# First two quads of a fused attention and MoE kernel as eight plain block products in two halves of tokens

## The chip, the cores and the metric

The kernel runs on one core of a Trainium2 chip. The metric is device time in microseconds (us), the median of three runs. The engines are named as in the profile: PE (TensorE, matrix products) with PEld (its weight loads), DVE (VectorE), ACT (ScalarE), POOL (GpSimd) and SP (SyncE, which here issues nearly all transfers).

## The reference

Three stages follow each other: attention with pooled keys and values, a dense mixture of four experts, and a gated layer with a norm. The inputs q, k, v have the shape (4, 8, 576, 64); there are 2304 tokens of width 512.

```python
def _attn_ref(q, k, v):
    k_p = k.reshape(B, H, Sp, pool, D).mean(axis=3)      # pool = 8, Sp = 72
    v_p = v.reshape(B, H, Sp, pool, D).mean(axis=3)
    scores = scale * np.matmul(q, k_p.transpose(0, 1, 3, 2))
    attn = softmax(scores)          # written out in the reference
    return np.matmul(attn, v_p)

def _moe_ref(x, domain_probs, w1, w2):   # E, F = 4, 1024
    p = domain_probs / (domain_probs.sum(-1, keepdims=True) + 1e-09)
    for e in range(E):
        h = np.maximum(x @ w1[e], 0.0)
        out += p[:, e:e + 1] * (h @ w2[e])

def _moe2_ref(x, w_gate, w_val, w_out, rms_g):   # d_ff = 1536
    xn = x / rms * rms_g
    g = xn @ w_gate
    return (g * sigmoid(g) * (xn @ w_val)) @ w_out
```

(The softmax and the sigmoid are shortened here.)

## The kernel before

**Tokens.** The 2304 tokens are 18 tiles of 128, worked on in three passes of six tiles. Each pass has two halves of N = 384 tokens, A and B.

**Products.** Every float32 operand is split into a high part (rounded by ScalarE to the format fp32r) and a low part (the rest, by VectorE), and a product is three matmuls: high by high, high by low, low by high (L462 to L464).

**Quads.** A quad is one block of 256 inner columns of an expert's first layer: 16 a pass. The 512 x 256 weights and the 768 tokens of a pass are each cut into 2 x 2 blocks (weights B11, B12, B21, B22; tokens a11 and a12 are the two halves of the width for token half A, a21 and a22 for B). `quad` (L441) makes the quad with seven block products instead of eight, by the table `STEPS`: sums of operands (s1 to s4 of tokens, T1, T2, N3, N4 of weights) go in, and sums of products come out. A product is six matmuls 128x384, so a quad is 42. The sums of tokens are made by `x_ops` once a pass, those of weights by `prep_w` (L253) once a quad, on GpSimd. After the products `relu_after` writes the hidden layer h of either half, high and low again.

**Second layer.** `second` (L777) takes a pair of quads and makes, for each of the six token tiles, 12 matmuls 128x512 with the pair's two rows of w2 (`prep_w2`, L308). These 72 are taken in pieces of three as a side queue between the products of the next quads.

**Hooks.** After each of a quad's seven products a hook runs: it takes the next piece of the side queue, the next step of the weight preparation, a tick that lets due stores go, and `att_step`, which runs the attention work written for this step. `when(i)` gives the step at which tile i of passes 1 and 2 begins; a tile's scores with exponentials (`att_a`), normalisation (`att_b`), transposes (`att_c`) and value products (`att_d`) follow at 0, 4, 8 and 13 steps from there. In that phase they all use one PSUM buffer of two banks (tag "at").

**First pass.** The attention of pass 0's six tiles runs before any quad, in the order 0, 3, 1, 4, 2, 5, with dummy products (`heat`) on TensorE. Its PSUM pool (two score buffers, three transpose banks, one dummy bank) is released before the quads' pool is opened. The token operands are made in thirds of columns, a third when both tiles of it (one of each half) are there.

The order of the instructions on each engine is the order of the program text; there is no scheduler.

Of the kernel before, what the change touches and what calls it, by code (L numbers as in the profile page):

```python
# [54 lines left out]
def tile_kernel(ctx: ExitStack, tc, qp, kp, vp, dp, w1r, w2r, w64, rg, out):  # L55
# [61 lines left out]
    def x_ops(c0=0, c1=N, new=True):  # L117

        a11, a12, a21, a22 = (xr[o, d][:, :, c0:c1] for o in (0, N) for d in range(2))

        if new:
            for _, _, _, name in STEPS:
                new_xo(name)

        def high(name, src):
            nc.scalar.activation(xo[0][name][:, 0, :, c0:c1], src, AF.Copy)

        def low(name, src):
            t = xo[0][name]
            nc.vector.tensor_tensor(t[:, 1, :, c0:c1], src, f32(t[:, 0, :, c0:c1]), op=ALU.subtract)  # L130
# [3 lines left out]

        add(a21, a11, ALU.subtract)
        high("a11", a11)
        yield
        low("a11", a11)
# [4 lines left out]
        high("a22", a22)  # L143
        yield
        add(a11, a21, ALU.add)
        high("s2", a21)
        high("a12", a12)
        yield
        low("s2", a21)
        low("a22", a22)  # L150
        high("s1", a11)
        yield
        low("a12", a12)
        low("s1", a11)
        add(a12, a21, ALU.subtract)
# [4 lines left out]
        yield  # L160
# [135 lines left out]


# [143 lines left out]
    def quad(i, after):  # L441
# [8 lines left out]
        seeded = i > 0  # L450
# [29 lines left out]
    def new_h(half, key):  # L480
        t = late["sb"].tile([P, 2, 2, N], F32R, name="h" + half, tag="h" + half, bufs=4 if half == "A" else 3)
        h_t[half, key] = t
        return t

# [292 lines left out]
    def second(keys, first, last):  # L777

        k, p, e, _ = keys[0]
        for t in (3, 4, 5, 0, 1, 2):  # L780
# [103 lines left out]
    def load_q(i):  # L884
# [8 lines left out]
        nc.sync.dma_start(t, qp[i].rearrange("p (j s) -> p j s", j=NPAIR))  # L893
# [9 lines left out]
    def pool_k(b, j, stage=None, eng=None):  # L903
# [41 lines left out]
    def heat(k):  # L945

        if "heat" not in at:
            at["heat"] = at["ps"].tile([P, 512], F32, name="heat")
        for _ in range(k):
            nc.tensor.matmul(at["heat"][:, :P], ident, ident, start=True, stop=True)  # L950
# [41 lines left out]
    def att_c(i):  # L992
# [6 lines left out]
        both = at["ps"].tile([P, 2, 512], F32, name="tr", tag="at") if at["few"] else None  # L999
        tr = [both[:, a] if at["few"] else at["ps"].tile([P, 512], F32, name="tr", tag="tr", bufs=3) for a in range(2)]  # L1000
        for h in range(H):
            nc.tensor.transpose(tr[h // 4][:SP, h % 4 * P:(h % 4 + 1) * P], es[:, h, :], ident)
        for a in range(2):
            src = tr[a][:SP, :].rearrange("p (h s) -> p h s", h=4)
            if a and not at["few"]:
# [5 lines left out]
    def att_d(i):  # L1011
        aT = aT_t.pop(i)
        if at["few"]:
# [12 lines left out]
        if p == 0:  # L1026
            for d in range(2):
# [312 lines left out]
```

## Time and profile before

| what | us |
|---|---|
| median of three runs | 1278.65 (1277.1 to 1281.29) |
| profiled execution | 1276.43 |
| its span | 1274.1 |
| TensorE busy | 1247.5 (98%) |
| VectorE busy | 828.2 (65%) |
| ScalarE busy | 535.4 (42%) |
| GpSimd busy | 268.7 (21%) |

The busy time of an engine is the union of its instructions. Matmuls are pipelined: the length of one in the trace (0.33 us for 128x384) overlaps the next, and the spacing of starts is what it costs. The span is that of the instructions, and the time of the execution contains a little beside it. PEclk is the clock that TensorE was granted, as a share of 2.4 GHz.

### The profile page before, as it was taken

The page shows a single profiled execution, that of the slowest core. Times are in us where ns is not written, and L with a number is a line of the kernel's source. Part 1 is how long each engine was busy: PE and PEld are TensorE (multiplying, and loading weights), DVE is VectorE, ACT ScalarE, POOL GpSimd, SP SyncE. Part 2 cuts the span into 40 slices and gives each one's busy share as a digit, 9 for nine tenths or more (in the row PEclk, how much of TensorE's full clock was granted, in tenths as well). Part 3 has the DMA queues.
Part 4 walks back from the last instruction along what each step waited for, and adds up shares of the span by engine and source line. Part 5 has one row for each costly group of instructions (what it writes and reads, how often), then busy time and mean ns, then how long its engine had stood idle before and what let it go on. Part 6 is the DMA issues. An engine that isn't in the chain of part 4 may idle for free.

```text
span 1274.1 us, 18396 instructions
## 1 busy us (share of the span) xinstructions
PE 1247.5 (98%) x6872; PEld 1153.5 (91%) x6872; DVE 828.2 (65%) x1340; ACT 535.4 (42%) x1239; POOL 268.7 (21%) x253
## 2 busy tenths in 40 slices
PE   7899999999999999999999999999999999999998
PEld 6788888888988888888889998888999999999998
DVE  5864556557466676645677787475667765786575
ACT  5674444444453333323443333255454433433331
POOL 5335333410031222200242343122220000000000
PEclk8899999999999999999999999999999999999999
DMA  8297777768788786664989998747877776867671
GB/s 248 85 340 278 276 252 248 286 236 313 277 309 281 258 286 255 233 246 168 330 312 332 325 326 314 281 177 274 328 263 277 279 293 254 313 242 295 233 275 50
DMA packets 118937, 339.15 MB, mean 266 GB/s; under 512 B 10304, under 2 KB 48192, under 8 KB 99648
## 3 DMA queue, kind: packets, MB, share of 16 engines
q1 hardware_dynamic: 118512, 336.80, 73.0%
q10 hardware_dynamic: 336, 1.18, 0.3%
q8 instruction: 54, 0.88, 0.3%
q14 instruction: 35, 0.29, 0.1%
HBM read 233.61 MB, written 104.33 MB: 265 GB/s over the span
## 4 chain that ended last, share of the span: by engine, by line
PE 84%; DVE 8%; DMA 4%; ACT 2%; issue 1%; SPq 0%; DVEq 0%; ACTq 0%
PE py L788 9%; PE py L789 9%; PE py L787 9%; PE qX L462 8%; PE qX L464 8%; PE qX L463 8%; PE qY L462 4%; PE qY L463 4%; PE qY L464 4%; PE qZ L462 2%; PE qZ L464 2%; PE qZ L463 2%; DMA wc_d<-cx 2%; PE gy L734 1%; PE gx L667 1%; PE av L1020 1%
## 5 line engine op out<-in xcount | busy, mean ns | idle before, releaser
L799 DVE SCALAR_TENSOR_TENSOR y<-py,dps,y 128x512 f32<-128x512 f32 x126 | 94.4, 749 | 186.4 <-PE py L789 186.3
L377 POOL TENSOR_TENSOR cx<-cx 128x512 f32<-128x512 f32 x36 | 49.8, 1383 | 380.4 <-DVE cx L376 91.2
L462 PE MATMUL qX<-xos,wt 128*128 128x384 f32 x336 | 116.2, 346 | 5.1 <-ACT s L470 3.5
L464 PE MATMUL qX<-xos,wt 128*128 128x384 f32 x336 | 113.6, 338 | 0.0
L789 PE MATMUL py<-w,hB 128*128 128x512 f32 x288 | 113.5, 394 | 0.0
L789 PE MATMUL py<-w,hA 128*128 128x512 f32 x288 | 113.4, 394 | 0.0
L788 PE MATMUL py<-w,hB 128*128 128x512 f32 x288 | 113.3, 393 | 0.0
L788 PE MATMUL py<-w,hA 128*128 128x512 f32 x288 | 113.2, 393 | 0.0
L463 PE MATMUL qX<-xos,wt 128*128 128x384 f32 x336 | 113.1, 337 | 0.0
L787 PE MATMUL py<-w,hB 128*128 128x512 f32 x288 | 112.0, 389 | 0.0
L787 PE MATMUL py<-w,hA 128*128 128x512 f32 x288 | 112.0, 389 | 0.0
L491 ACT ACTIVATE hB<-u 128x768 fp32r<-128x768 f32 x48 | 40.8, 850 | 139.3 <-DVE u L474 139.2
L273 POOL TENSOR_TENSOR tw<-rw 128x512 f32<-128x512 f32 x28 | 41.3, 1474 | 263.0 <-DVE wt L291 192.0
L470 ACT ACTIVATE s<-qX 128x384 f32<-128x384 f32 x85 | 41.6, 490 | 120.3 <-PE qX L464 120.2
L467 ACT ACTIVATE qZ<-qX 128x384 f32<-128x384 f32 x83 | 39.8, 480 | 120.5 <-PE qX L464 82.6
L472 DVE TENSOR_TENSOR u<-qY,s 128x384 f32<-128x384 f32 x84 | 46.5, 553 | 56.5 <-PE qY L464 27.2
L462 PEld LDWEIGHTS qX<-xos,wt 128*128 128x128 f32 x336 | 63.3, 188 | 13.2 <-ACT s L470 5.8
L463 PEld LDWEIGHTS qX<-xos,wt 128*128 128x128 f32 x336 | 63.3, 189 | 2.9
L789 PEld LDWEIGHTS py<-w,hB 128*128 128x128 f32 x288 | 54.0, 188 | 11.5
L789 PEld LDWEIGHTS py<-w,hA 128*128 128x128 f32 x288 | 54.0, 188 | 11.4
L464 PEld LDWEIGHTS qX<-xos,wt 128*128 128x128 f32 x336 | 63.1, 188 | 0.2 <-DVE wt L291 0.2
L788 PEld LDWEIGHTS py<-w,hA 128*128 128x128 f32 x288 | 54.0, 188 | 10.1
(188 smaller groups left out, 3499.4 us busy)
## 6 DMA issues: line engine op xcount, KB each, us to landing
wt<-wt_d SPq DMA_DIRECT2D x56, 1024.0 KB, 7.4
w<-w_d SPq DMA_DIRECT2D x32, 1024.0 KB, 8.6
wt_d<-wt SPq DMA_DIRECT2D x28, 1024.0 KB, 7.3
wr<-wr_d SPq DMA_DIRECT2D x56, 512.0 KB, 8.0
wr_d<-wr SPq DMA_DIRECT2D x28, 768.0 KB, 5.9
cr<-w SPq DMA_DIRECT2D x36, 512.0 KB, 7.1
w<-ws_d SPq DMA_DIRECT2D x18, 1024.0 KB, 5.8
w_d<-w SPq DMA_DIRECT2D x16, 1024.0 KB, 9.0
```

Source lines behind the costliest of these rows:

```text
L273: nc.gpsimd.tensor_tensor(t[:, T1:N3 + 1], r[:, B12:B12 + 1].to_broadcast([P, 2, 256]), r[:, B11:B22 + 1], op=sub)
L377: nc.gpsimd.tensor_tensor(x, x, m.bitcast(F32), op=ALU.mult)
L462: nc.tensor.matmul(bank[b], wh, xh, start=first and k == 0, stop=False, **kw)
L463: nc.tensor.matmul(bank[b], wh, xl, start=False, stop=False, **kw)
L464: nc.tensor.matmul(bank[b], wl, xh, start=False, stop=k == 1, **kw)
L470: nc.scalar.activation(s[n], bank[b], AF.Copy)
L472: nc.vector.tensor_tensor(u[:, 0], bank["Y"], s[2], op=ALU.add)
L491: nc.scalar.activation(h[:, 0], u, AF.Relu)
L787: nc.tensor.matmul(ps, lhs[0], w[:, 0, c], start=j == 0, stop=False)
L788: nc.tensor.matmul(ps, lhs[0], w[:, 1, c], start=False, stop=False)
L789: nc.tensor.matmul(ps, lhs[1], w[:, 0, c], start=False, stop=j == len(units) - 1)
L799: nc.vector.scalar_tensor_tensor(y_t[t], ps, gate, y_t[t], op0=ALU.mult, op1=ALU.add)
```

## The change

Quads 0 and 1 are no longer made by `quad` but by eight plain block products each, four for either half of the tokens, in `by_half(i, h, c)`: quad i, half h, column block c. The plain products need no sums. The tiles of attention come in the order 0 to 5, so that half A is whole after three tiles; `att_d` writes the split operands directly from PSUM. Half A's four products and its second layer (tiles 0, 1, 2 of `second`) are written between the stages of tiles 3 to 5, then come half B's four products, two more tiles of the second layer, and quad 2. The PSUM pool is now opened after the first exponentials of tile 3, and in this stretch transposes and values use the quads' banks qY and qZ ("few" is 2). The token sums are made whole (`x_rest`) and no longer in thirds, the weight sums of quads 0 and 1 in pieces. The small copies of the second batch's pooled keys move from ScalarE to GpSimd. As 14 hooks fewer are left, the pass-1 tiles follow each other after 13 steps instead of 16. The core of the diff:

```diff
+    def by_half(i, h, c):
+        w = wop[i]
+        key = quads[i]
+        o = h_t.get(("AB"[h], key)) if c else new_h("AB"[h], key)
+        ps = late["ps"].tile([P, 512], F32, name="qX", tag="qX", bufs=2)[:, :N]
+        blocks = ((B11, B21), (B12, B22))[c]
+        for j, (name, slot) in enumerate(zip((("a11", "a12"), ("a21", "a22"))[h], blocks)):
+            for k in range(2):
...
+                nc.tensor.matmul(ps, wh, xh, start=j == k == 0, stop=False)
+                nc.tensor.matmul(ps, wh, xl, start=False, stop=False)
+                nc.tensor.matmul(ps, wl, xh, start=False, stop=j == k == 1)
+        def out():
+            nc.scalar.activation(o[:, 0, c], ps, AF.Relu)
+            nc.vector.scalar_tensor_tensor(
+                o[:, 1, c], ps, 0.0, f32(o[:, 0, c]), op0=ALU.max, op1=ALU.subtract
+            )
+        return out
-        seeded = i > 0
+        seeded = i > 2
...
-                    nc.scalar.activation(kpb[b % 2][sl, j + i, hh, :], c[sl], AF.Copy)
+                    if b:
+                        nc.gpsimd.tensor_copy(o, c[sl])
+                    else:
+                        nc.scalar.activation(o, c[sl], AF.Copy)
...
-        if at["few"]:
+        if at["few"] == 2:
+            av = late["ps"].tile([P, 512], F32, name="av", tag="qY")
+        elif at["few"]:
             av = at["ps"].tile([P, 2, 512], F32, name="av", tag="at")[:, 0]
...
+            for d in range(2):
+                nc.scalar.activation(ops[d][:, 0, :, sl], avv[:, 2 * d:2 * d + 2], AF.Copy, scale=1.0 / POOL)
+            for d in range(2):
+                nc.vector.scalar_tensor_tensor(
+                    ops[d][:, 1, :, sl], avv[:, 2 * d:2 * d + 2], 1.0 / POOL, f32(ops[d][:, 0, :, sl]),
+                    op0=ALU.mult, op1=ALU.subtract,
+                )
...
+    by_half(0, 0, 0)()
+    o = by_half(0, 0, 1)
+    att_b(3)
+    att_sc(4)
+    first_high(1)
+    first_low(1)
+    att_c(3)
+    o()
+    gates()
+    att_ex(4)
+    o = by_half(1, 0, 0)
+    att_d(3)
...
+    att_b(4)
+    att_sc(5)
+    o = by_half(1, 0, 1)
...
+    att_ex(5)
+    run(two[:1], 4)
+    load_w2(rows[1])
+    att_d(4)
+    tick()
+    py = second(pair, True, False, range(TT))
+    run(two[1:], 5)
+    att_b(5)
+    for _ in range(4):
+        next(py)
+    att_c(5)
...
-        return (p - 1) * NSTEP + 2 + 16 * t
+        return NSTEP - 12 + 16 * t if p > 1 else 2 + 13 * t
```

The instructions of TensorE where the block products of the first quads begin, in the kernel before: `heat` are dummy products, `tr` the transposes and `av` the value products of the last tiles, `qX` the first product of quad 0.

```order
L950 MATMUL heat<-ident 128x128 x10
L1002 MATMUL tr<-ident,es 72x128 x8
L1020 MATMUL av<-aT,vpb_90 64x128 x8
L1020 MATMUL av<-aT,vpb_93 64x128 x8
L950 MATMUL heat<-ident 128x128 x4
L462 MATMUL qX<-xoa_385,wr 128x384
L463 MATMUL qX<-xoa_385,wr 128x384
```

The same place on TensorE in the changed kernel: the transposes and value products are those of tile 2, the third.

```order
L1076 MATMUL tr<-ident,es 72x128 x8
L1017 MATMUL heat<-ident 128x128 x4
L1096 MATMUL av<-aT,vpb_90 64x128 x8
L1017 MATMUL heat<-ident 128x128 x6
L535 MATMUL qX<-xoa_187,wr 128x384
L536 MATMUL qX<-xoa_187,wr 128x384
```

The first products have moved ahead of the attention of tiles 3 to 5, of which only the scores of tile 3 stand before them.

VectorE in the changed kernel, around the second row of w2: `w_562` and `w_643` are the low parts of the first and second row, `xoa` the low parts of tile 4's operands, L1055 to L1057 tile 5's normalisation, L1080 the copy of its transposes.

```order
L359 TENSOR_TENSOR w_562<-rw_179,w_562 128x512
L1108 SCALAR_TENSOR_TENSOR xoa_194<-av,xoa_194 128x2x128
L1108 SCALAR_TENSOR_TENSOR xoa_190<-av,xoa_190 128x2x128
L359 TENSOR_TENSOR w_643<-rw_616,w_643 128x512 x2
L1055 TENSOR_SCALAR sm<-sm 128x8
L1056 RECIPROCAL sm<-sm 128x8
L1057 TENSOR_TENSOR es<-es,sm 128x576
L1080 COPY aT<-tr 72x512
```

Before, all of the attention of pass 0 stands ahead of the w2 parts on VectorE; now the last tile's normalisation stands behind those of the second row.

TensorE in pass 1 before, where the value products of a tile end: `qX` and `qY` are products of a quad, `py` the second layer.

```order
L1020 MATMUL av<-aT,vpb_93 64x128 x8
L462 MATMUL qX<-xos_387,wt 128x384
L463 MATMUL qX<-xos_387,wt 128x384
L464 MATMUL qX<-xos_387,wt 128x384
L462 MATMUL qX<-xos_387,wt 128x384
L463 MATMUL qX<-xos_387,wt 128x384
```

The same in the changed kernel, at one of five such places: `sc` are the scores of the next tile.

```order
L502 MATMUL qX<-xos_193,wr 128x384
L1096 MATMUL av<-aT,vpb_93 64x128 x8
L1032 MATMUL sc<-kpb_88,q 128x144 x4
L500 MATMUL qX<-xoa_187,wr 128x384
L501 MATMUL qX<-xoa_187,wr 128x384
```

The scores, which stood two products and a piece of the second layer further on, now stand directly behind the value products, both on the buffer "at".

## Rows read from the trace of the kernel before

**Rows 1.** The page: busy time of each engine.
```profile
PE 1247.5 (98%) x6872; PEld 1153.5 (91%) x6872; DVE 828.2 (65%) x1340; ACT 535.4 (42%) x1239; POOL 268.7 (21%) x253
```

**Rows 2.** Windows from 77.76 to 330 us: sum of busy time by engine.
```profile
sum 252.24, PE 252.08 PEld 225.41 DVE 145.29 ACT 118.70 POOL 77.56; mean PE 36.01 PEld 32.20 DVE 20.76 ACT 16.96 POOL 11.08
```

**Rows 3.** TensorE timeline: start, length (us), line, operation; the quads' first matmuls.
```profile
50.64 1.16 PE L950 MATMUL heat<-ident 128*128 128x128 f32 x8
...
54.08 0.69 PE L462 MATMUL qX<-xoa,wr 128*128 128x384 f32 x1 [2.28 <-ACT xoa L126]
...
66.32 0.33 PE L462 MATMUL qX<-xoa,wr 128*128 128x384 f32 x1
...
77.76 0.33 PE L462 MATMUL qX<-xoa,wr 128*128 128x384 f32 x1
...
78.80 0.33 PE L462 MATMUL qY<-xos,wt 128*128 128x384 f32 x1
```

**Rows 4.** TensorE timeline: scores, transposes and second layer of the first quads.
```profile
60.66 1.14 PE L965 MATMUL sc<-kpb,q 128*128 128x144 f32 x8
...
61.54 0.43 PE L462 MATMUL qY<-xoa,wt 128*128 128x384 f32 x1
...
73.73 1.04 PE L1002 MATMUL tr<-ident,es 128*72 128x128 f32 x8 [1.62 <-DVE es L990]
...
74.53 0.42 PE L462 MATMUL qX<-xos,wt 128*128 128x384 f32 x1
...
85.90 0.39 PE L787 MATMUL py<-w,hB 128*128 128x512 f32 x1
...
88.67 0.33 PE L462 MATMUL qX<-xos,wt 128*128 128x384 f32 x1
```

**Rows 5.** ScalarE timeline: first and sixth tile's exponentials.
```profile
13.66 0.32 ACT L981 ACTIVATE es<-sc,m 128x72 f32<-128x72 f32 x1 [2.00 <-DVE m L975]
...
41.56 0.32 ACT L981 ACTIVATE es<-sc,m 128x72 f32<-128x72 f32 x1
...
43.93 0.61 ACT L1008 ACTIVATE aT<-tr 72x512 f32<-72x512 f32 x1
```

**Rows 6.** Windows (length; PE, PEld, DVE, ACT, POOL; PEclk; DMA share; GB/s), then TensorE timeline.
```profile
57.00:58.00 1.00, 1.00 (x4) 1.00 (x4) 1.00 (x4) 0.00 (x0) 0.00 (x0) 0.50 0.00 0
...
60.00:61.00 1.00, 1.00 (x7) 1.00 (x7) 0.98 (x1) 0.25 (x2) 0.95 (x1) 0.90 0.62 262
...
57.69 0.52 PE L462 MATMUL qY<-xos,wt 128*128 128x384 f32 x1
...
58.01 0.52 PE L463 MATMUL qY<-xos,wt 128*128 128x384 f32 x1
```

**Rows 7.** SyncE, ScalarE, VectorE timelines: loads of w2, high and low parts.
```profile
70.03 0.33 SPq L305 DMA_DIRECT2D rw<-w2r  x1
...
79.54 0.33 SPq L305 DMA_DIRECT2D rw<-w2r  x1
...
74.31 0.63 ACT L319 ACTIVATE w<-rw 128x512 fp32r<-128x512 f32 x1 [2.73 <-DMA rw<-w2r]
...
87.31 0.63 ACT L319 ACTIVATE w<-rw 128x512 fp32r<-128x512 f32 x1 [1.70 <-DMA rw<-w2r]
...
58.84 0.68 DVE L291 TENSOR_TENSOR wt<-tw,wt 128x512 fp32r<-128x512 f32 x1
```

**Rows 8.** VectorE and GpSimd timelines: the normalising multiply.
```profile
46.86 0.76 DVE L990 TENSOR_TENSOR es<-es,sm 128x576 f32<-128x576 f32 x1
...
33.29 1.54 DVE L990 TENSOR_TENSOR es<-es,sm 128x576 f32<-128x576 f32 x1
...
32.96 2.46 POOL L898 TENSOR_TENSOR stg<-stg 72x512 f32<-72x512 f32 x2
```

**Rows 9.** TensorE and ScalarE timelines: value products of a pass-1 tile, their eviction.
```profile
121.90 1.09 PE L1020 MATMUL av<-aT,vpb 72*64 72x128 f32 x16
...
122.92 0.44 PE L462 MATMUL qX<-xos,wt 128*128 128x384 f32 x1
...
123.04 0.60 ACT L1034 ACTIVATE st<-av 128x512 f32<-128x512 f32 x1 [3.25 <-PE av L1020]
```

More of the change, by code (lines that the diff above doesn't have):

```diff
@@ L775, in new_y, with second @@
         return late["sb"].tile([P, HT * DM], F32, name="y", tag=f"y{half}")
-    def second(keys, first, last):
+    def second(keys, first, last, tiles=(3, 4, 5, 0, 1, 2)):
         k, p, e, _ = keys[0]
-        for t in (3, 4, 5, 0, 1, 2):
+        for t in tiles:
             half, sl = "AB"[t // HT], slice(t % HT * P, t % HT * P + P)
@@ L948, in heat @@
             at["heat"] = at["ps"].tile([P, 512], F32, name="heat")
+        t = late["ps"].tile([P, 512], F32, name="heat", tag="py", bufs=2) if at["few"] else at["heat"]
         for _ in range(k):
-            nc.tensor.matmul(at["heat"][:, :P], ident, ident, start=True, stop=True)
+            nc.tensor.matmul(t[:, :P], ident, ident, start=True, stop=True)
     def att_a(i):
@@ L1049, in tile_kernel, with run @@
             xr[o, d] = t[:, d]
-    order = (0, 3, 1, 4, 2, 5)
-    def run(queue, k=1):
+    def run(queue, k=1, one=False):
         for _ in range(k):
@@ L1058, in run @@
                 queue.pop(0)
+                if one:
+                    break
+    rows = [q for q in quads if q[0] == "m"]
+    side = []
     k0 = [pool_k(0, j, "hA", nc.vector) for j in (0, 2)]
-    v0 = [
-        pool_v(0, h, t, e, nc.scalar)
-        for h, t, e in ((0, "hA", None), (2, "hB", None), (4, "hB", None), (6, None, None))
-    ]
-    load_q(order[0])
-    next(k0[0])
-    next(k0[1])
-    for it in v0:
+    v0 = [pool_v(0, h, t, e) for h, t, e in ((0, "hA", None), (2, "hB", None), (4, "hB", None), (6, None, nc.vector))]
@@ new lines, in tile_kernel @@
+    for i in range(3, TT):
+        load_q(i)
+    load_w2(rows[0])
+    for it in v1[:3]:
+        next(it)
+    first_xo()
+    open_w(0)
+    open_w(1)
+    att_sc(0)
+    att_sc(1)
+    first_high(0)
+    att_ex(0)
+    next(v0[3])
+    next(v1[3])
+    heat(20)
+    att_ex(1)
+    att_b(0)
+    att_sc(2)
+    att_c(0)
+    att_b(1)
+    att_sc(3)
+    att_ex(2)
+    first_low(0)
+    first_sums(0)
+    load_w(1)
+    att_c(1)
+    att_d(0)
+    att_b(2)
+    att_d(1)
+    heat(4)
+    att_c(2)
@@ new lines, in tile_kernel @@
+    heat(4)
+    att_d(2)
+    att_ex(3)
+    for it in k1 + v1:
+        next(it)
+    heat(6)
+    psa.release()
+    late["ps"] = tc.alloc_tile_pool(name="psl", bufs=1, space=bass.MemoryType.PSUM)
+    at["ps"] = tc.alloc_tile_pool(name="psb", bufs=1, space=bass.MemoryType.PSUM)
+    at["few"] = 2
+    nc.sync.dma_start(g_bc, rg.to_broadcast([P, DM]))
+    load_q(TT)
+    load_q(TT + 1)
+    two = [prep_w2(rows[0]), prep_w2(rows[1])]
+    pair = [quads[0], quads[1]]
+    by_half(0, 0, 0)()
+    o = by_half(0, 0, 1)
@@ new lines, in tile_kernel @@
+    att_c(5)
+    for _ in range(4):
+        next(py)
+    att_d(5)
+    tick()
+    rest = [first_rest(0), first_rest(1)]
+    run(rest, 2, True)
+    for _ in range(4):
+        next(py)
+    run(rest, 1, True)
+    first_sums(1)
+    load_w(2)
+    xit = [x_rest()]
+    wit = iter(())
+    for i in range(2):
+        for c in range(2):
+            o = by_half(i, 1, c)
+            run(xit)
+            o()
+            run(rest)
+            tick()
+        if not i:
+            load_w2(rows[2])
@@ L1122, in tile_kernel @@
+    wit = prep_w(2)
+    for t in range(2):
+        for _ in range(4):
+            next(py)
+            run(xit)
             next(wit, None)
-    heat(4)
+            tick()
     run(xit, 30)
@@ L1126, in tile_kernel @@
         pass
[L1127 to L1133 removed]
+    at["few"] = 1
     NSTEP = 7 * E * R1
@@ L1176, in tile_kernel @@
         stages[-1][1].append(i)
-    def row_of(i):
-        k, p, e, r = quads[i]
-        return (k, p, e, r) if k == "m" else None
-    rows = [row_of(i) for i in range(NQ) if row_of(i)]
-    nrow = [0]
+    nrow = [2]
     def prep_row():
```

177 lines of the change are left out of this document (92 added, 85 removed).

## The prediction

> **What bounds the kernel now.** I read the page's busy table first: TensorE is busy for 98% of the span [rows 1], so its time is the currency of this kernel, and only stretches in which it stands still or runs at the lower clock can be won. Then I cut the span into windows. From 77.76 us, where the third quad begins, to 330 us TensorE is busy 252.08 of 252.24 us [rows 2]: from there on nothing is to be gained, and every new wait costs its full length. Ahead of 77.76 us lies the attention of the first six tiles, where TensorE waits and is filled with dummy products. The TensorE timeline gives the marks: the first block product of quad 0 starts at 54.08 us after 2.28 us of idle, quad 1 at 66.32, quad 2 at 77.76 us [rows 3]. Quad 1 takes 11.44 us (77.76 − 66.32), although its 42 matmuls at 0.1735 us each (six in 78.80 − 77.76 = 1.04 us, [rows 3]) are 7.3 us and the transposes among them 0.8: some 3.3 us are waits.
>
> The change touches two stretches: the one up to quad 2, and the attention of pass 1 inside the saturated stretch. Each gets its own sum.
>
> **Break-even: when must quad 2 start?** After the change, 60 of the 72 second-layer matmuls of the first pair stand ahead of quad 2; before, all 72 stand behind it. One costs 0.231 us (twelve from 85.90 to 88.67 us, [rows 4]), so 60 × 0.231 = 13.86 us of saturated work are then done. On the other side, the scores (60.66 to 61.54, 0.88 us) and the transposes of tile 6 (73.73 to 74.53, 0.80 us), which before lie ahead of quad 2, are still to come. The change breaks even if quad 2 starts at 77.76 + 13.86 − 0.88 − 0.80 = 89.9 us, provided that all behind it runs as before. The 12 additional matmuls (96 plain against 84) cost 12 × 0.1735 = 2.1 us, and lie inside that time.
>
> **When does it start?** I follow the chain by hand, from durations of before.
>
> *To the first block product.* Its PSUM bank lies where score buffers were, so it waits for the exponentials of tile 3, the fourth tile. In before the first exponential starts at 13.66 us, and the sixth tile's eight run from 41.56 to 43.93 us [rows 5]: (43.93 − 13.66) / 6 = 5.04 us a tile, 2.37 of them exponentials. Four tiles give 13.7 + 4 × 5.04 = 33.9 us; the two column blocks of quad 0's operands that come between add a little: 34.5. Lower bound 31, if the missing operand sums (made tile by tile in before) shorten each tile by 0.7 us; upper 36, if the low parts, now tied tile by tile to ScalarE's evictions, lengthen it.
>
> *The 24 products of quad 0's first half.* At full clock 24 × 0.1735 = 4.2 us. But TensorE has stood still ahead of them, only a few dummy matmuls on its queue. In before, after an idle 2.28 us, the granted clock is 0.50 (1.2 GHz) in the window from 57 us and one matmul takes 0.32 us (58.01 − 57.69); it is back at 0.90 between 60 and 61 us [rows 6], about 6 us in all. I take 2.4 us for such a spell here: 34.5 + 4.2 + 2.4 = 41.1.
>
> *Tiles 4 and 5.* Scores 0.9, then about 2.0 until ScalarE can start (its wait for the maxima in [rows 5]), exponentials 2.4: tile 4's end at 46.4 us. The score buffer is single in this stretch, so tile 5's scores can only start then, and take the same 5.3 us: 51.7. Beside them run the other 24 first-half products (4.2 us), the transposes and value products; they are hidden here, and so are the weight parts of quad 1.
>
> *The second layer's weights.* The load of w2's second row reuses the single raw buffer, and so is issued only after VectorE has made the second low part of the first row. ScalarE's high part of that stands behind tile 5's exponentials, and VectorE's low parts behind the relu remainders: I take 56 us, from 52.5 at the least to 58. From issue to the first high part the trace has 4.3 us (70.03 to 74.31) and, beside other transfers, 7.8 us (79.54 to 87.31) [rows 7]. I take the first, as the queue has little else. Two highs of 0.63 and a low of 0.68 us (that of a weight part of the same shape, [rows 7]) follow: 56 + 4.3 + 1.26 + 0.68, so the second layer's seventh matmul, the first on that row, can run at about 62.2 us. Behind this wait on VectorE stand tile 5's normalisation, and behind TensorE's own wait the transposes of tile 5: nothing covers the hole.
>
> *From there to quad 2.* 60 × 0.231 + 48 × 0.1735 (the second half's products) + 0.8 + 1.0 (transposes and values of tile 5) = 24.0 us, less the six matmuls done before the hole (1.4), 1.9 us for one more spell at the lower clock after it, and 2.3 us, two thirds of what quad 1 lost in before, for products that stand behind VectorE and ScalarE: 62.2 + 22.6 + 1.9 + 2.3 = **89.0 us**. Ends: 80 if the load comes 6 us sooner and the clock stays, 96 if the load takes 7.8 us and VectorE's steps grow.
>
> How much they may grow, a row shows: the normalising multiply takes 0.76 us alone (46.86) and 1.54 us at 33.29, with GpSimd's 2.46 us of adding beside it [rows 8]. The change puts more on GpSimd in just this stretch: beside its pooling of the second batch's values it makes eight small copies of that batch's keys that were ScalarE's. The Trainium skill ("SBUF — State Buffer", "Who interferes with whom") speaks against this: VectorE and GpSimd share a port pair as an exclusive lock, and a VectorE instruction with two SBUF inputs blocks against a GpSimd one that reads SBUF. By that rule, the doubling of this row is what it says, and each normalisation of tiles 1 to 3 and each low part there would wait; taken fully it gives the late end above.
>
> **Behind the start of quad 2.** In before, quad 1 lost 3.3 us to ScalarE and VectorE order. In the changed kernel quads 2 and 3 are the first of the old kind, quad 2 without the copy of its first product into the third bank, and with the operands s3, s2, s1 and s4 and its own weights just made: I take 1.5 us, from 0 to 5.
>
> **The new wait in pass 1.** The pass-1 tiles now follow each other every 13 hooks, and the value products of one tile and the scores of the next fall into the same hook. Both use the one PSUM buffer of two banks, so the scores wait until ScalarE has evicted the values. Before, three or more hooks of other matmuls lay between. The order shows this at five places (tiles 6/7 to 10/11). Price: in before the value products that began at 121.90 give way to the next matmul at 122.92, and the eviction runs from 123.04 for 0.60 us to 123.64 [rows 9], so the scores could start some 0.8 us after TensorE is free; nothing stands ahead of them on TensorE that could fill it. With one weight part of 0.63 us in ScalarE's way it is 1.4 us, with nothing in the way no less than 0.7. Five times 0.8 = 4.0 us; ends 3.5 and 11 (two parts and an eviction each time, 2.2 us). Since the stretch is saturated, all of it counts. Behind the waiting scores stand the next quad's products and everything else on TensorE.
>
> **Sum.** 89.0 − 89.9 + 1.5 + 4.0 = +4.6 us. The profiled execution took 1276.4 us, 2.2 us below the median of the three timed runs, 1278.65. On the median: 1278.65 + 4.6 = **1283.3 us**. About 0.3% (3.8 us) is the least that a measurement of this kernel can tell from no change: faster means below 1274.8, slower above 1282.5.
>
> **Rivals.**
> *No change: ScalarE is in time for the scores.* If the values' eviction is over before the scores come up (TensorE's sequencer, or other matmuls that the trace puts between), the five waits vanish: 89.0 − 89.9 + 1.5 = +0.6, so 1279.3 us. For it: ScalarE is only half busy in [rows 2]. Against it: the eviction cannot start before the value products end, and nothing stands between. A start of quad 2 at 86 us with the waits kept gives nearly the same, 1280.3.
> *Faster: the hole at w2's second row is not there.* The first row's low parts are made as soon as that row has landed, ahead of tile 5's exponentials, the load goes out at 50 us, and the second layer starts at about 55 instead of 62; without the hole the clock stays up, which gives back 1.9 us: quad 2 at 89.0 − 7 − 1.9 = 80, and 80 − 89.9 + 1.0 + 4.0 = −4.9, so 1273.8 us. For it: the exponentials themselves are only 2.4 of the 5 us a tile, and TensorE has 16.7 + 13.9 us of real work ready from 34.5 us on. Against it: the high part is written behind those exponentials on ScalarE's queue. It decides where the gap ahead of the second layer is under 2 us.
> *Much slower: GpSimd and the clock.* VectorE's steps in tiles 1 to 5 double as at 33.29 us, the block products run at the lower clock throughout, quad 2 starts at 95: 95 − 89.9 + 2 + 4.5 = +11.6, so 1290.3 us.
>
> **How the numbers follow.** The forecast case (1281 to 1288) 0.45, no change 0.25, faster 0.20, much slower 0.10. Of the forecast case about a fifth, 0.09, lies below 1282.5. Slower: 0.36 + 0.10 = 0.46, less 0.02 for its lower edge, 0.44; same: 0.25 + 0.09 = 0.34; faster: 0.20 + 0.02 = 0.22. The range of 8 in 10 reaches from 1272 (most of the faster case) to 1290 (the edge of the much slower one); the forecast case's own is 1281 to 1288.
>
> **What would show it.** The first plain product near 34.5 us, with a granted clock near 0.5 behind it; a gap of several us on TensorE that ends with VectorE's low part of the second w2 row, near 62 us; quad 2 near 89 us; and five waits of about 0.8 us on the scores, each put down to ScalarE's eviction. If quad 2 starts ahead of 83 us, the chain by hand is too long and the change wins; if the scores do not wait, the second sum falls; if TensorE is at the higher clock from 34 to 60 us, both spells do.

## The result

The changed kernel takes 1289.86 us (median of five runs, 1289.16 to 1295.72) against 1278.65 for the kernel before: 11.2 us more, and the ratio of the means is 1.0095 with a 95% interval of 1.007 to 1.012. The forecast was 1283.3, slower by 4.6 us. The direction was right; the size was not, by more than a factor of two. The median lies just inside the range of 8 in 10 (1272 to 1290), and above the forecast case's own (1281 to 1288).

The profiled execution took 1295.72 us, with a span of 1293.9. That is the longest of the five, 19.8 us of span above the profiled execution of before. So I use a second profile of the same changed kernel, taken later, beside it (span 1290.4). The one trace of before is, on the other hand, of an execution 2.2 us below its median.

The page's busy table after, which answers to [rows 1]:

```profile
PE 1253.2 (97%) x6872; PEld 1155.5 (89%) x6872; DVE 828.0 (64%) x1328; ACT 532.0 (41%) x1224; POOL 269.3 (21%) x258
```

TensorE is busy for 5.7 us longer (1253.2 against 1247.5), of which the 12 added matmuls are 2.1; the number of matmuls is the same, as 12 records of dummies fell away. The other 14.1 of the 19.8 us are idle time: 0.3 ahead of quad 2, 6.7 between quads 2 and 4, 5.1 from there to quad 16, and 2.0 behind it.

The TensorE timeline of the changed kernel (columns as in [rows 3]), from the first block product to quad 2:

```profile
36.12 0.44 PE L535 MATMUL qX<-xoa,wr 128*128 128x384 f32 x1 [3.12 <-ACT es L1048]
...
37.86 0.53 PE L537 MATMUL qX<-xoa,wr 128*128 128x384 f32 x1
...
38.18 0.53 PE L535 MATMUL qX<-xoa,wr 128*128 128x384 f32 x1
...
42.07 1.20 PE L1032 MATMUL sc<-kpb,y 128*64 128x144 f32 x16
...
63.16 0.80 PE L849 MATMUL py<-w,hA 128*128 128x512 f32 x1 [3.62 <-ACT w L357]
...
89.22 0.33 PE L500 MATMUL qX<-xoa,wr 128*128 128x384 f32 x1
```

The first plain product waits for tile 3's exponentials, tile 4's scores follow at 42.07, the second row of w2 holds the second layer until 63.16, and quad 2 begins at 89.22 us. In between the spacing of two matmuls is 0.32 us (38.18 − 37.86), the lower clock of [rows 6], after 3.12 us of idle.

The hole ahead of 63.16, on SyncE's queue and on ScalarE (answers to [rows 7]):

```profile
58.28 0.33 SPq L343 DMA_DIRECT2D rw<-w2r  x1
...
62.47 1.15 ACT L357 ACTIVATE w<-rw 128x512 fp32r<-128x512 f32 x2 [2.86 <-DMA rw<-w2r]
```

The load is issued at 58.28 and ScalarE's high part starts 4.2 us later.

Behind quad 2, TensorE waits five times until 111 us:

```profile
90.60 0.44 PE L502 MATMUL qX<-xoa,wr 128*128 128x384 f32 x1 [0.87 <-DVE wr L274]
...
97.77 0.44 PE L500 MATMUL qX<-xos,wt 128*128 128x384 f32 x1 [1.40 <-ACT s L508]
...
101.70 0.44 PE L500 MATMUL qX<-xos,wr 128*128 128x384 f32 x1 [1.55 <-DVE u L512]
...
106.26 0.44 PE L500 MATMUL qX<-xos,wt 128*128 128x384 f32 x1 [1.17 <-ACT qZ L505]
...
110.26 1.04 PE L1076 MATMUL tr<-ident,es 128*72 128x128 f32 x8 [1.62 <-DVE es L1057]
```

In before TensorE was busy throughout the stretch that answers to it [rows 2]; its own quads 0 and 1 had three of the same kind, 0.25 us on VectorE's sum of products `u`, 1.16 on the copy of quad 1's first product and 1.62 on the normalised exponentials ahead of the transposes [rows 4]. New are 0.87 us at 90.60, on the low part of quad 2's own weights, and 1.40 at 97.77; the wait on `u` has grown to 1.55. SyncE and ScalarE show where the one at 97.77 is from:

```profile
90.62 0.33 SPq L243 DMA_DIRECT2D rw<-w1r  x1
...
96.49 0.84 ACT L272 ACTIVATE wr<-rw 128x768 fp32r<-128x768 f32 x1 [2.71 <-DMA rw<-w1r]
...
97.24 0.47 ACT L508 ACTIVATE s<-qX 128x384 f32<-128x384 f32 x1
```

Quad 3's weights are loaded only at 90.62 us and land at 96.49. ScalarE's high part of them stands ahead of the copy of quad 2's product (97.24), for which TensorE waits.

From 113 to 330 us the view of waits (total, times, longest) lists the scores and hardly anything else:

```profile
PE sc L1032 <- ACT st L1118: 4.3, 4, 2.2
...
PE sc L1032 <- issue: 0.7, 1, 0.7
```

The longest of them, with ScalarE's queue ahead of the eviction `st<-av`, then TensorE:

```profile
254.19 0.84 ACT L553 ACTIVATE hB<-u 128x768 fp32r<-128x768 f32 x1 [4.06 <-DVE u L512]
...
254.94 0.61 ACT L282 ACTIVATE wt<-tw 128x512 fp32r<-128x512 f32 x1
...
255.46 0.61 ACT L357 ACTIVATE w<-rw 128x512 fp32r<-128x512 f32 x1
...
255.98 0.57 ACT L1118 ACTIVATE st<-av 128x512 f32<-128x512 f32 x1
...
253.30 1.09 PE L1096 MATMUL av<-aT,vpb 72*64 72x128 f32 x16
...
256.61 1.81 PE L1032 MATMUL sc<-kpb,q 128*128 128x144 f32 x6 [2.22 <-ACT st L1118]
```

The values end at about 254.3, but ScalarE has a relu part and two weight parts to do first, and the eviction starts only at 255.98. Behind it the granted clock falls from 1.00 (windows: length; busy time of PE, PEld, DVE, ACT, POOL; granted clock; DMA share; GB/s):

```profile
250.00:260.00 10.00, 7.78 (x46) 6.86 (x45) 3.63 (x8) 2.50 (x6) 2.43 (x3) 0.79 0.77 267
...
260.00:270.00 10.00, 10.00 (x44) 8.80 (x43) 3.64 (x6) 5.10 (x21) 3.15 (x3) 0.87 0.22 59
```

**How late the changed kernel is, and from where on.** The starts of the same quad in two timelines give the lag. Quad 2: 89.22 − 77.76 = 11.5 us. Quad 4: 117.05 − 112.10 = 4.95. Quad 16, the first of the next pass, by when the attention of pass 1's tiles is done in both: 330.03 − 313.89 = 16.1. Of what changes sides, 60 second-layer matmuls take 13.86 us off the lag up to quad 4. The order of the attention pieces takes off another 1.0 (ahead of quad 4, before has the values of tile 6 and the scores and transposes of tile 7, 2.7 us, between quads 2 and 4; the changed kernel has there those of tile 6, 1.7 us), and puts the 2.7 back behind it. So quads 2 and 3 lost 14.9 − 6.5 = 8.4 us, and the stretch from quad 4 to 16 lost 11.2 − 2.7 = 8.5. In the second profile these are 8.3 and 5.6 us, since there the clock did not fall behind the longest wait.

All these lags are against the one trace of before. The kernel of experiment 2 below has before's order on TensorE up to quad 2 and reached it 2.55 us later, so a lag is good to some 2 or 3 us; the difference of two marks within one trace says more.

One more piece lies in neither stretch. Between quads 32 and 36, where the third pass begins, the lag grows by 3.5 us (2.8 in the second profile). The longest wait there, in before and in the changed kernel:

```profile
629.33 0.44 PE L462 MATMUL qX<-xos,wt 128*128 128x384 f32 x1 [0.87 <-ACT s L470]
...
647.39 0.45 PE L500 MATMUL qX<-xos,wt 128*128 128x384 f32 x1 [2.74 <-ACT s L508]
```

This wait is 0.65 to 3.14 us in the seventeen profiles of this case: 0.65 in experiment 6, whose order there is the changed kernel's, and 3.14 in experiment 2, whose order there is that of before. So I put it down to the execution and not to the change; that is argued and not shown.

### The profile page after: what moved, and what is told of

The parts are those of the page before. It is cut to its first block, busy times and chain, and to the rows that moved or that the text cites. A ratio compares the mean times of both kernels' runs of the same rounds, so it can differ in the third digit from the quotient of the medians.

```text
span 1293.9 us, 18380 instructions
## 1 busy us (share of the span) xinstructions
PE 1253.2 (97%) x6872; PEld 1155.5 (89%) x6872; DVE 828.0 (64%) x1328; ACT 532.0 (41%) x1224; POOL 269.3 (21%) x258
## 4 chain that ended last, share of the span: by engine, by line
PE 78%; DVE 8%; DMA 5%; ACT 3%; issue 1%; SPq 1%; POOL 0%; ACTq 0%; DVEq 0%
PE py L850 8%; PE py L851 8%; PE py L849 8%; PE qX L500 8%; PE qX L502 7%; PE qX L501 7%; PE qY L500 4%; PE qY L501 4%; PE qY L502 4%; PE qZ L500 2%; PE qZ L502 2%; PE qZ L501 2%; DMA wc_d<-cx 2%; PE gy L796 1%; PE gx L729 1%
## 5 line engine op out<-in xcount | busy, mean ns | idle before, releaser
L500 PE MATMUL qX<-xos,wt 128*128 128x384 f32 x328 | 113.2, 345 | 8.3 <-ACT s L508 6.8
L849 PE MATMUL py<-w,hA 128*128 128x512 f32 x288 | 113.8, 395 | 4.6 <-ACT w L357 4.6
L850 PE MATMUL py<-w,hA 128*128 128x512 f32 x288 | 114.6, 398 | 0.1
L851 PE MATMUL py<-w,hA 128*128 128x512 f32 x288 | 114.3, 397 | 0.0
L502 PE MATMUL qX<-xos,wt 128*128 128x384 f32 x328 | 110.9, 338 | 0.0
L501 PE MATMUL qX<-xos,wt 128*128 128x384 f32 x328 | 110.3, 336 | 0.0
L508 ACT ACTIVATE s<-qX 128x384 f32<-128x384 f32 x83 | 40.6, 489 | 113.2 <-PE qX L502 112.9
L266 POOL TENSOR_TENSOR tw<-rw 128x512 f32<-128x512 f32 x26 | 37.9, 1457 | 233.0 <-DVE wt L284 182.6
L500 PEld LDWEIGHTS qX<-xos,wt 128*128 128x128 f32 x328 | 61.6, 188 | 16.2 <-ACT s L508 8.8
L849 PEld LDWEIGHTS py<-w,hA 128*128 128x128 f32 x288 | 54.8, 190 | 15.9 <-ACT w L357 5.8
L851 PEld LDWEIGHTS py<-w,hA 128*128 128x128 f32 x288 | 54.7, 190 | 11.6
L850 PEld LDWEIGHTS py<-w,hA 128*128 128x128 f32 x288 | 54.7, 190 | 11.1 <-DVE w L359 1.0
L851 PEld LDWEIGHTS py<-w,hB 128*128 128x128 f32 x288 | 54.2, 188 | 11.5
L501 PEld LDWEIGHTS qX<-xos,wt 128*128 128x128 f32 x328 | 61.6, 188 | 2.8
```

The costliest lines, as they stand in the source:

```text
L500: nc.tensor.matmul(bank[b], wh, xh, start=first and k == 0, stop=False, **kw)
L501: nc.tensor.matmul(bank[b], wh, xl, start=False, stop=False, **kw)
L502: nc.tensor.matmul(bank[b], wl, xh, start=False, stop=k == 1, **kw)
L508: nc.scalar.activation(s[n], bank[b], AF.Copy)
L849: nc.tensor.matmul(ps, lhs[0], w[:, 0, c], start=j == 0, stop=False)
L850: nc.tensor.matmul(ps, lhs[0], w[:, 1, c], start=False, stop=False)
```

## The experiments

All medians are of runs beside the kernel before on the same chip, whose median lay between 1277.7 and 1279.2 us. "Lag" is the start of a quad against that in the trace of before.

| kernel | median us | ratio of the means to before, 95% interval | quad 2 at | lag quad 4 | lag quad 16 |
|---|---|---|---|---|---|
| changed, first runs | 1289.86 | 1.0095 [1.007, 1.012] | 89.22 | 4.95 | 16.14 |
| changed, second runs | 1292.45 | 1.0107 [1.0092, 1.0122] | 89.06 | 4.73 | 13.04 |
| values one step sooner | 1287.64 | 1.0071 [1.0056, 1.0086] | 89.01 | 4.69 | 7.33 |
| the same, second runs | 1285.50 | 1.0050 [1.0037, 1.0063] | 89.79 | 5.22 | 7.85 |
| before, tiles every 13 steps | 1284.25 | 1.0060 [1.0038, 1.0082] | 80.31 | 3.59 | 9.73 |
| w2 early | 1284.62 | 1.0052 [1.0037, 1.0066] | 82.83 | −2.75 | 7.22 |
| weight sums early | 1289.60 | 1.0088 [1.007, 1.0107] | 90.55 | 2.88 | 12.86 |
| 34 dummies | 1296.92 | 1.0141 [1.0122, 1.0159] | 92.32 | 8.30 | 16.64 |
| 20 dummies | 1293.66 | 1.0114 [1.0092, 1.0135] | 91.02 | 6.45 | 14.79 |
| 20 dummies, second runs | 1294.14 | 1.0116 [1.0101, 1.0131] | 89.44 | 5.18 | 15.13 |
| key copies on ScalarE | 1292.39 | 1.0111 [1.0092, 1.013] | 88.94 | 5.00 | 13.33 |
| values, w2, sums | 1281.99 | 1.0022 [1.001, 1.0034] | 86.61 | −1.08 | 1.55 |
| values, w2, dummies | 1281.03 | 1.0011 [0.9999, 1.0023] | 83.87 | −2.01 | 0.62 |
| values, w2, sums, dummies | 1281.66 | 1.0015 [1.0001, 1.0028] | 82.62 | −5.12 | −2.49 |
| values, w2, sums later | 1280.57 | 1.0020 [1.0009, 1.0031] | 86.83 | −0.92 | 1.73 |
| values, w2 | 1278.29 | 0.9998 [0.9989, 1.0007] | 86.56 | 0.67 | 3.27 |

**1. The wait on the scores, taken away.**

```diff
-        for o, f in ((0, att_a), (4, att_b), (8, att_c), (13, att_d)):
+        for o, f in ((0, att_a), (4, att_b), (8, att_c), (12, att_d)):
```

> Changed kernel, but each tile's value products one step earlier (12 steps after its scores, not 13), so that they no longer stand directly ahead of the next tile's scores. Theory (the scores wait for ScalarE's eviction of the values on the one shared buffer): the five waits on the scores, 0.7 us four times and 2.2 us once in the changed kernel's profile, go, and with them the spell of lower clock behind the longest, about 3 us: 5 to 8 us less, 1282 to 1285. Rival (ScalarE is behind anyway, and what waits is only moved to the next products): the same waits on other matmuls, within 1 us of the changed kernel.

The values now stand a product and some matmuls of the second layer ahead of the scores. In the TensorE timeline the same tile's values, the product behind them, and the next tile's scores, which do not wait:

```profile
117.93 1.09 PE L1096 MATMUL av<-aT,vpb 72*64 72x128 f32 x16
...
118.95 0.44 PE L500 MATMUL qY<-xos,wt 128*128 128x384 f32 x1
...
122.89 1.15 PE L1032 MATMUL sc<-kpb,q 128*128 128x144 f32 x8
```

No wait is left from 113 to 330 us, and between quads 4 and 16 the lag grows by 2.64 us, just the 2.7 of attention that changes sides. Against 11.2 and 8.3 us in the two profiles of the changed kernel, the waits and what comes with them are 5.7 to 8.5 us in the traces. The median fell by 2.2 us only (5 to 8 were expected), and the two kernels had not run beside each other, so I ran both once more, side by side:

> The changed kernel once more, unaltered, beside the two others of this call on the same chip. Theory: 11 to 12 us slower than before, as in its first runs; in its profile quad 2 at 89 to 90 us, 6 to 7 us of idle up to quad 4, five waits on the scores of 5 us together. The spell of lower clock at 250 us comes and goes between executions.

> The kernel with the values one step sooner once more. Theory (the five waits are worth their 5 us): 4 to 6 us below the changed kernel of the same call. Rival (its first runs' 2.2 us are all, because the clock takes the rest back): 1.5 to 3 us below, with a spell of lower clock near 100 us in its profile again.

There the difference is 1292.45 − 1285.50 = 7.0 us, beyond the upper end of what was expected; the changed kernel itself was 13.7 us above before, 2 more than expected. The two comparisons leave 2 to 7 us for the medians. That the first runs had lost the rest to the clock isn't shown: both profiles have their spells of lower clock, at different places.

**2. The same wait, put into the kernel before.**

```diff
-        return (p - 1) * NSTEP + 2 + 16 * t
+        return NSTEP + 2 + 16 * t if p > 1 else 2 + 13 * t
```

> Kernel before, with nothing changed but the spacing of the pass-1 tiles, 13 steps instead of 16. Theory: the price of the shared buffer by itself: five waits of 0.7 to 0.8 us, 3.5 to 4 us slower than before, more if a wait is long enough for the clock to fall. Rival (the waits come from the changed order around the first quads, not from the spacing): within 1 us of before.

1284.25 against 1277.69 us: 6.6 us slower by the spacing alone, with the quads as they were, where the waits by themselves had been expected to cost 3.5 to 4. Its five waits on TensorE are 0.97, 0.70, 0.74, 0.70 and 2.22 us. The first and the longest, which is as long as that of the changed kernel:

```profile
87.31 0.88 PE L965 MATMUL sc<-kpb,q 128*128 128x144 f32 x5 [0.97 <-ACT st L1034]
...
220.09 1.86 PE L965 MATMUL sc<-kpb,q 128*128 128x144 f32 x8 [2.22 <-ACT st L1034]
```

From quad 2 to 16 its lag grows by 7.2 us: 5.3 of waits, and behind the longest a granted clock of 0.83 from 220 to 230 us. By this measure the spacing is the larger half of the 11.2 us, and it needs none of the plain products.

**3. Both rows of w2 early.** The first row's parts go ahead of the first product, the second row's load behind them, its parts behind tile 4's exponentials; tile 5's transposed scores get another buffer (`if i < TT - 1` in `att_c`):

```diff
+    run(two[:1], 6)
+    load_w2(rows[1])
     by_half(0, 0, 0)()
...
-    next(two[0])
+    run(two[1:], 2)
...
-    next(two[0])
+    run(two[1:], 4)
...
-    run(two[:1], 4)
-    load_w2(rows[1])
...
-    run(two[1:], 5)
```

> Changed kernel, but both rows of w2 for the first pair prepared in idle places: the first row's parts ahead of the first block product, the second row's load right behind, its parts behind tile 4's exponentials (tile 5's transposed scores get another buffer for that). Theory (the hole at 57 to 63 us is the load of the second row, and the lower clock behind it is its consequence): no wait of over 1.5 us ahead of the second layer, quad 2 at 80 to 82 us instead of 89.2; 6 to 8 us less if the next quads keep pace. Rival (weight sums and loads of quads 2 and 3 bound as well): quad 2 comes sooner only by 2 to 4 us or loses it again in quads 2 and 3, 0 to 3 us less.

The load's issue, ScalarE's high parts of the second row, the second layer's first tile, and quad 2:

```profile
39.72 0.33 SPq L343 DMA_DIRECT2D rw<-w2r  x1
...
51.51 1.16 ACT L357 ACTIVATE w<-rw 128x512 fp32r<-128x512 f32 x2
...
56.72 0.50 PE L849 MATMUL py<-w,hA 128*128 128x512 f32 x1
...
82.83 0.33 PE L500 MATMUL qX<-xoa,wr 128*128 128x384 f32 x1
```

The hole is gone, and quad 2 begins 6.4 us sooner. The median falls by 5.2 us against the first runs (7.8 against the second). So the early load pays; but as the waits behind quad 2 and on the scores stay, the kernel is still slower than before.

**4. Weight sums early.** Quad 0's sums are split ahead of the first product, quad 1's are formed as soon as its plain parts are there and split in the hole, and quad 2's load follows them.

```diff
+    rest = [first_rest(0), first_rest(1)]
+    run(rest[:1], 4)
     by_half(0, 0, 0)()
...
     first_low(1)
+    first_sums(1)
+    load_w(2)
     att_c(3)
...
+    run(rest[1:], 4)
     run(two[1:], 5)
...
-    rest = [first_rest(0), first_rest(1)]
```

> Changed kernel, but the weight sums' parts of quad 0 made ahead of the first block product, the sums of quad 1 right behind its plain parts, those of its parts in the hole at 59 us, and quad 2's weights loaded from there. Theory (quads 2 and 3 lose 6.5 us because quad 3's weights are loaded only at 90.6 us and ScalarE's high part of them stands ahead of the quads' copies): the waits from 89 to 112 us shrink to about 2 us, 4 us less in all, 1285 to 1286. Rival (the loss is that of two quads that begin on empty buffers, with the exponentials in ScalarE's way, as quad 1 had in before, 3.3 us): 0 to 1.5 us less.

The waits behind quad 2 that are left on TensorE:

```profile
99.62 0.44 PE L500 MATMUL qX<-xos,wr 128*128 128x384 f32 x1 [1.52 <-DVE u L512]
...
104.18 0.45 PE L500 MATMUL qX<-xos,wt 128*128 128x384 f32 x1 [1.16 <-ACT qZ L505]
...
108.17 1.04 PE L1076 MATMUL tr<-ident,es 128*72 128x128 f32 x8 [1.63 <-DVE es L1057]
```

Those on the late weights are gone, and the three that remain are of the kind that quads 0 and 1 had in before (0.25, 1.16 and 1.62 us). From quad 2 to 4 the lag falls by 9.9 instead of 6.5 us: 3.4 us, as the theory has it, and it leaves 5.0 of the 8.4. But the moved work cost time ahead of quad 2: it came 1.5 us later than in the second profile of the changed kernel, whose first product began at the same 37.79 us. The median, 1289.60, is 0.3 below the changed kernel's first runs and 2.9 below its second; 4 were expected. So late weights are 3.4 us of the loss. For the other 5.0 the rival theory (two quads that begin on empty buffers) is only borne out by the kind of the three waits, 4.3 us together; no run takes them away.

**5. Dummies against the lower clock.**

```diff
-    heat(6)
+    heat(34)
```

> Changed kernel with 34 dummy products instead of 6 ahead of the first block product, so that TensorE is not idle from 33.0 to 36.1 us. Theory (the idle lowers the clock from 37.3 to 40.7 us, in which one matmul takes 0.32 us instead of 0.17): that spell goes, the first 24 products take 4.2 instead of 6 us, and the chain behind them comes 1.5 to 2 us sooner: quad 2 near 87.3 us, 1.5 to 2 us less in all. Rival (the chain behind is set by ScalarE and VectorE, not by these products): quad 2 within 0.5 us of 89.2, no change.

My dose was too large: one dummy takes 0.23 us, and the last ended at 40.8 us. Tile 4's scores and quad 2 both came 3.1 us later than in the changed kernel: here what delayed tile 4 delayed quad 2 one for one. With 20:

> Changed kernel with 20 dummy products instead of 6 ahead of the first block product: 34 ran 3.5 us past the exponentials, and by 0.23 us each 20 end at 36.0, where the first block product began. Theory (the 3.1 us of idle lower the clock of the first products): no spell from 37 to 41 us, tile 4's scores at 40.5 instead of 42.1 us, and quad 2 earlier by the same 1.5 us: 1288. Rival (the lower clock comes anyway and only later): quad 2 within 0.5 us of 89.2, or later; 1289 to 1291.

This was slower too. As its profile began with keys that landed 2 us late, I ran it again:

> The kernel with 20 dummy products once more. Theory (its first profile's keys landed 2 to 4 us late by chance): its first block product at 36 us and quad 2 near 87.5 us, 1 to 2 us below the changed kernel of the same call. Rival (the dummies do cost): 2 us or more above it, with the first block product near 40 us again.

The dummies (two records each), tile 4's scores, the second layer's wait and quad 2 in that second profile, and two windows, the first of the changed kernel, the second of this one:

```profile
32.07 4.73 PE L1017 MATMUL heat<-ident 128*128 128x128 f32 x40
...
41.27 1.20 PE L1032 MATMUL sc<-kpb,y 128*64 128x144 f32 x16
...
62.67 0.79 PE L849 MATMUL py<-w,hA 128*128 128x512 f32 x1 [4.33 <-ACT w L357]
...
89.44 0.33 PE L500 MATMUL qX<-xoa,wr 128*128 128x384 f32 x1
...
60.00:70.00 10.00, 6.84 (x23) 5.20 (x24) 3.02 (x6) 2.43 (x4) 0.00 (x0) 0.60 0.77 303
...
60.00:70.00 10.00, 7.33 (x22) 5.49 (x23) 3.03 (x6) 2.43 (x4) 0.00 (x0) 0.54 0.72 294
```

There is no spell from 37 to 41 us and the scores come 0.8 us sooner; but the wait for w2 (4.33 us against 3.62 and, in the second profile of the changed kernel, 4.19) and the spell behind it, which the changed kernel has as well (granted clock 0.54 from 60 to 70 us, against 0.60 and 0.66), take it back, and quad 2 is where it was. Nor is it shown that the dummies kept the clock up: in the second profile of the changed kernel it is 1.00 from 30 to 50 us without them (with 0.68 from 20 to 30, against 0.83 in the first), and its quad 2 is at 89.06 all the same. Why the median is 1.7 to 3.8 us above the changed kernel's I can't say.

**6. Key copies on ScalarE again** (undoes one part of the change).

```diff
-                    if b:
-                        nc.gpsimd.tensor_copy(o, c[sl])
-                    else:
-                        nc.scalar.activation(o, c[sl], AF.Copy)
+                    nc.scalar.activation(o, c[sl], AF.Copy)
```

> Changed kernel with the eight key copies of the second batch on ScalarE again. Theory (GpSimd's part beside VectorE costs nothing here: its pooling from 36 to 48 us lengthens VectorE's steps by under 1 us, and the copies are 2.4 us of it): ScalarE's eight copies stand behind tile 3's exponentials, where it idles for 3.4 us, so no change within 1 us. Rival (the shared work of GpSimd and VectorE is what holds tiles 4 and 5): 1 to 3 us less, with the normalisation and the low parts from 40 to 48 us back at their durations alone (0.76 and 0.95 us).

VectorE's low parts of quad 1's weights, with GpSimd's pooling now over by 37 us (in the changed kernel it begins only behind the copies, at 36.3):

```profile
44.58 0.96 DVE L308 TENSOR_TENSOR wr<-rw,wr 128x768 fp32r<-128x768 f32 x1
...
45.45 0.42 DVE L309 TENSOR_TENSOR wb<-rw,wb 128x256 fp32r<-128x256 f32 x1
```

The same two in the changed kernel, and GpSimd's pooling beside them:

```profile
44.22 1.23 DVE L308 TENSOR_TENSOR wr<-rw,wr 128x768 fp32r<-128x768 f32 x1
...
45.37 1.50 DVE L309 TENSOR_TENSOR wb<-rw,wb 128x256 fp32r<-128x256 f32 x1
...
44.59 2.87 POOL L960 TENSOR_TENSOR vr<-vr 72x512 f32<-72x512 f32 x2
```

The smaller of them takes 1.50 us beside GpSimd and 0.42 alone, the larger 1.23 and 0.96. A lengthening like that of [rows 8] is there, as the prediction feared, and by the Trainium skill's rule that it cited (SBUF — State Buffer, Who interferes with whom) the trace agrees. But no cost of it shows: without it quad 2 is at 88.94 instead of 89.22 and 89.06, and the median, 1292.39, is not lower.

**7. The cures together.** First three of them:

> Changed kernel with the three cures together: values one step sooner, both w2 rows early, weight sums early. Theory (the three losses lie one behind the other on TensorE and add up): quad 2 at 81 to 83 us, waits of about 2 us up to quad 4, no waits on the scores: 13 to 15 us less than the changed kernel, 1274 to 1277, level with the kernel before or up to 3 us faster. Rival (VectorE and ScalarE have no room for all of it ahead of quad 2, as the work is only moved): quad 2 at 86 us or later, 1280 to 1284.

1281.99, 7.9 us below the changed kernel, and not the 13 to 15 expected: quad 2 came at 86.6, not 81 to 83, as the rival had it. With dummies instead of the sums, and with all four:

> Changed kernel with the values one step sooner, both w2 rows early, and 20 dummy products. Theory: the first two are worth 2.2 and 5 us by themselves and lie one behind the other, the dummies 1.5: quad 2 at 81 to 82 us, no wait on the scores, 1279 to 1281, 0 to 2 us above the kernel before. Rival (what is saved goes to the clock): spells of lower clock between 40 and 110 us in the profile that the single runs did not have, 1282 to 1285.

> As the kernel with three, and the weight sums of quad 0 and those of quad 1 early, but quad 1's parts left behind tile 5, since they had stood ahead of its normalisation. Theory: quad 2 as with three, waits of quads 2 and 3 about 3 us less, 1276 to 1278. Rival (the early parts delay tiles 4 and 5 again): quad 2 at 84 us or later, 1280 to 1284.

Both are within 1 us of the three cures: 1281.03, at the upper end of what its theory had, and 1281.66, in the range of its rival, although its quad 2 came at 82.6.

Then the sums at another place, and only the two cures that had helped by themselves:

> The three cures without dummies, the weight parts of quad 0 now behind tile 3's normalisation (not ahead of the first product), those of quad 1 behind tile 5. Theory: quad 2 at 81 to 83 us, quads 2 and 3 lose 3 us less than in the changed kernel, no waits on the scores: quad 4 at 106 to 107 us, 1276 to 1279, level with the kernel before. Rival (the early weight parts cost tiles 4 and 5 as much as they save): no better than the two cures alone.

> Changed kernel with two cures: values one step sooner and both w2 rows early. Theory (the two terms add): the changed kernel less 5 to 6 for the w2 rows and 5 to 6 for the waits, 1279 to 1282; quad 2 at 82 to 84, quad 4 at 109 to 110 us. Rival (one cures the other): 1284 or more, no better than the w2 rows alone.

Two cures have the lowest median: 1278.29 us, ratio 0.9998 [0.9989, 1.0007], level with the kernel before and a little under what was expected (1279 to 1282). Against the kernel with dummies instead (1.0011 [0.9999, 1.0023]) the intervals overlap. Quad 2 in its profile, and the window from 113 to 330 us, saturated again:

```profile
86.56 0.33 PE L500 MATMUL qX<-xoa,wr 128*128 128x384 f32 x1
...
113.00:330.00 217.00, 217.00 (x1180) 194.26 (x1179) 132.54 (x198) 100.58 (x255) 72.10 (x73) 1.00 0.78 282
```

The early sums gain in the traces where they were meant to (lag at quad 4 of −0.92 against 0.67, with quad 2 at nearly the same time), but the median of that kernel is 2.3 us higher, and its runs spread from 1277.6 to 1284.2 us against 1277.8 to 1281.0. The starts show where the gain goes. The first product and the wait on the low parts of quad 1's weights, with the sums and then without:

```profile
37.91 0.44 PE L535 MATMUL qX<-xoa,wr 128*128 128x384 f32 x1 [3.12 <-ACT es L1048]
...
48.69 0.44 PE L537 MATMUL qX<-xoa,wr 128*128 128x384 f32 x1 [3.12 <-DVE wr L308]
...
40.59 0.44 PE L535 MATMUL qX<-xoa,wr 128*128 128x384 f32 x1 [3.12 <-ACT es L1048]
...
49.25 0.44 PE L537 MATMUL qX<-xoa,wr 128*128 128x384 f32 x1 [1.01 <-DVE wr L308]
```

The two kernels have the same order up to the first product; that it came 2.7 us later in the second is its execution, whose first exponentials came 2.6 us later already. Counted from there, quad 2 comes after 48.9 us with the sums and after 46.0 without: VectorE makes quad 0's weight parts ahead of quad 1's, and TensorE waits 3.12 instead of 1.01 us for those. Of the 2.9 us, 1.9 come back by quad 4. So the early sums cost tiles 4 and 5 a little more than they save behind quad 2, as the rival had it.

## Why the prediction was wrong

**The chain to quad 2 came out right, in part by luck.** First product 34.5 forecast, 36.1 measured; tile 4's scores 41.1 and 42.1; issue of w2's second row 56 and 58.3; from there to the first high part 4.3 and 4.2; the second layer's wait until 62.2 and 63.2; quad 2 at 89.0 and 89.2. In the eight profiles with that order the time from tile 4's scores to the second layer was 20.8 to 21.6 us; the forecast had 21.1. But inside these marks steps were wrong and cancelled. Tile 5's exponentials were to end at 51.7 us; on ScalarE they begin only later:

```profile
54.52 0.32 ACT L1048 ACTIVATE es<-sc,m 128x72 f32<-128x72 f32 x1
```

They end at 57.0 us, and the load, for which the forecast left 4.3 us more, goes out 1.3 us behind them. From the hole to quad 2 the waits on VectorE and ScalarE were 0.4 us and not 2.3. And in the second profile the first product came at 37.8 us, beyond the upper end of 36, with no spell of lower clock behind it, and tile 4's scores at 42.2 all the same.

**"Behind the start of quad 2 ... I take 1.5 us, from 0 to 5" is the step that failed.** It measured 8.4 and 8.3 us, beyond the upper end. I had scaled one quad's loss in before (3.3 us) down for two quads. Experiment 4 shows what I missed for 3.4 us of it: the weights of quads 2 and 3 come late in a row. Quad 1's sums wait for the buffer that quad 0's leave only at 76 us, quad 2's load waits for those sums, quad 3's for quad 2's, and ScalarE's part of quad 3 blocks a product's copy. I had followed the queue up to quad 2 and not the two loads behind it. The other 5.0 us are mostly three waits on VectorE and ScalarE of the kind that quads 0 and 1 had in before; what would take them away stays open.

**The waits on the scores were there, and under-priced.** Forecast 5 × 0.8 = 4.0 us; measured four of 0.70 to 0.74 and one of 2.22, together 5.0 us, and with restarts and, in one of two profiles, the clock, 5.6 to 8.5. The 2.22 is the upper end that I had named for one wait; a relu part and two weight parts of ScalarE stand ahead of that eviction.

With both terms as measured the sum is −0.7 + 8.4 + 5.6 to 8.5 = 13.3 to 16.2 us, against 13.0 and 16.1 of lag at quad 16. That is no check of the break-even, since the two losses were read from the same lags with the same 13.86 and 2.7 us; of these, experiment 1 bears out the 2.7 (2.64 where nothing waits). The medians differ by 11.2 and 13.7 us; the trace of before is of an execution 2.2 us below its median, the first one of the changed kernel 5.9 above its own.

**The rivals.** "ScalarE is in time for the scores" fell: all five waits are there. "The hole is not there" fell for the changed kernel, but its mechanism held in experiment 3: without the hole quad 2 comes at 82.8 (80 was forecast). "Much slower" got the time right (1290.3) by luck: quad 2 was not at 95, and no cost of GpSimd shows.

## What to carry to other kernels

In a stretch where one engine is saturated, look at what two neighbours in the program share: a buffer handed from one to the next costs its eviction each time (0.7 us, and 2.2 with others queued ahead), and here one step of distance hid it all. When work is moved ahead of a pipeline, follow the loads of the first stages behind the move as carefully as the move itself; each waits for the buffer of the one before. And work that is taken out of one wait may make another: weight parts moved ahead saved 1.9 us behind quad 2 and cost 2.9 ahead of it.

## What the runs showed of the hardware

Filling idle time with dummy matmuls did not pay here: with 20 dummies from 32.1 to 36.8 us the granted clock was 1.00 from 30 to 50 us, but so it was in one of two executions without them, and behind the next wait of 4.3 us it was 0.54 from 60 to 70, against 0.60 and 0.66 without. Two executions of one program had spells of lower clock that the other had not (37 to 41 and 250 to 270 us in one, 90 to 110 in the other, at 0.90 and 0.93) and were level at tile 4's scores (42.07 and 42.18 us). And the time from program start to the first block product differed by up to 4.5 us between executions of kernels whose order up to there is the same but for w2's parts (36.1 to 40.6 us), and by 4.1 us between two whose order is the same throughout (36.52 and 40.59), so marks from one profile are best read as differences from an early mark.
